# A decode kernel with two cached-attention passes: half of wq and a quarter of wo leave SBUF and are reread, and all 16 chunks of a row's last two units stay on chip between its passes

## The chip, the cores and the metric

The kernel runs on one core of one Trainium2 chip. The metric is the device time of one execution in microseconds (us). The kernel before takes 1079.54 us, the median of three runs (1079.27 to 1081.7). MB is 10^6 bytes, KB in the profile is 1024 bytes.

## What is computed

There are 8 rows (batch entries), each with one token of 448 values. The layers are attention, mixer, attention, mixer, each added to its input:

```python
x = x + A(layernorm(x), k_cache, v_cache, wq, wo)   # pass 0
x = x + B(layernorm(x), w1, w2, w3, w4)
x = x + A(layernorm(x), k_cache, v_cache, wq, wo)   # pass 1, the same caches and weights
x = x + B(layernorm(x), w1, w2, w3, w4)
```

`A` has 16 query heads of 256 and 8 KV heads, two query heads to each KV head, and 4096 cached positions: q = x @ wq, softmax(q k^T / 16) @ v, then @ wo. `B` adds gelu(layernorm(x1) @ w3) @ w4 to x1, where x1 = x + hs. With one token the shifts in `B` push out the only position, so hs is zero and w1 and w2 are not needed; the kernel leaves them out. Both attention passes read the same cache, so what stays on chip after pass 0 of a row need not be read again for pass 1.

## The kernel before, in words

**Units and chunks.** A *unit* is one row, one pass and one pair of KV heads (`gp`, 0 to 3), which serves four query heads. A unit has 4 K chunks and 4 V chunks; a chunk is 128 partitions of 8 KB, 1024 KB in all. So a row has 32 chunks in a pass. The units with gp 0 and 1 are called *free* (heads 0 to 7), those with gp 2 and 3 *kept* (heads 8 to 15).

**Places.** All chunks go through one SBUF tile, `places`, of NC = 15 places of one chunk each (L61, L77). `emit_loads` (L750) walks a fixed list of loads, in the order in which the chunks are used, and issues each on SP's DMA queue as soon as the plan has a place for it; two K chunks in neighbouring places go as one DMA of 2048 KB (L765), a single chunk as one DMA (L790), and a V chunk in `halved` as two DMAs of 512 KB (L793). SP is in order: a load whose place is still in use holds up the loads behind it.

**What stays.** Of the 16 chunks of a row's two kept units, 12 stay in their places from pass 0 to pass 1 (`kept`, L64). One more (`inner`) is moved to four PSUM banks by four VectorE transposes (`away`, L835) and back (`back`, L842), and a quarter of another (`part`) to a fifth bank (L1114, back at L1127), so that 768 KB of it are read again. The weights wq, wo, w3 and w4 are loaded once and stay in SBUF.

**The work on a chunk.** VectorE transposes a K chunk in place in three instructions (`transpose_k`, L803). TensorE makes scores from a pair of K chunks (`scores`, L818) into the PSUM bank `sc`: the first pair into columns 0 to 255, the second into 256 to 511. ScalarE takes the exponential of a pair (`exps`, L827). For a V chunk TensorE runs 16 matmuls (`pv`, L871). K chunks that stayed need no second transpose.

**Order of the work.** `first_kept` and the loop at L639 write the order out by hand, as a list of items, each one chunk. Per row b it is: pass 1 of the row's kept units; then, for the next row, a mix of free units ahead of their turn (`ahead`, L573, three or four units per row, from pass 0 of later rows and from pass 1 of earlier ones) and pass 0 of its two kept units. At the end of this, V chunks that are due (`AFTER` = 11 of them, in `narrow`) are worked one half at a time, and between the halves `step` (L930) advances the *chain* of the row (`chain`, L522): heads 8 to 15 through wo, mixer (`mlp`), and q for pass 1 (`project_q`, L323: 128 matmuls on wq for all 16 heads), after which pass 1 of the row's kept units can start. So the chain stage is the stretch in which only V chunks are worked, with three places left over, and the stretch after it has all K chunks of the row.

**q and wo.** q of pass 0 is projected once for all 8 rows. `spread_q` (L346) writes a row's q for all 16 heads into one of two tiles `qbd`. `first_half` (L512) takes heads 0 to 7 of a row's pass 0 through wo (64 matmuls). For pass 1, rows 0 to 3 go through wo and the mixer together (`rest`, L561), rows 4 to 7 at the end of the kernel (L1136 on).

Of the kernel before, what the change touches and what calls it, by code (L numbers as in the profile page):

```python
# [17 lines left out]
def kernel(  # L18
# [42 lines left out]
    NC = 15  # L61
# [3 lines left out]
    kept += [(GP - 1, 1, n) for n in range(1, 4)] + [(GP - 2, 1, 2)]  # L65
    inner = (GP - 2, 1, 1)
    part = (GP - 1, 1, 0)
    Q4 = 4 * Dh
# [9 lines left out]
    slots = [places_t[:, n * PB : (n + 1) * PB] for n in range(NC)]  # L78

# [50 lines left out]
    def room_ps(what, nb):  # L130

        at, n = {"y": (288, 8), "st": (296, 2), "h": (298, HC), "q": (288, NB2)}[what]
        if nb == 1:
            return misc[:, at : at + n]
        if nb < Bn:
            at = {"y": 352, "st": 384, "h": 400}[what]
            return misc[:, at : at + n * nb]
        at, n = {"y": (0, 8), "st": (64, 2), "h": (80, HC), "q": (256, NB2)}[what]
        return store[0][:, at : at + n * nb]
# [51 lines left out]
    wq_sb = split_tile(HD, "wq_sb")  # L191
    w3_sb = split_tile(F, "w3_sb")
    wo_sb = consts.tile([128, NB2, D], BF16, name="wo_sb")
    w4_sb = consts.tile([128, HC, D], BF16, name="w4_sb")
    qbds = [consts.tile([128, 8, GP, 4, 2], BF16, name=f"qbd{k}") for k in range(2)]
# [29 lines left out]
    def norm(x, nb, twice):  # L225
# [71 lines left out]
        if nb == 1:  # L297
            nc.vector.scalar_tensor_tensor(  # L298
                xbs(1)[:, 0:4, 0], xc[:, :, 0], rl, low[:, int(twice)], ALU.mult, ALU.mult
            )  # L300
            parts = parts[1:2]
        for p0, p1, x0, f0, f1, to in parts:
            pp = slice(x0, x0 + p1 - p0)
            dst = xbs(nb)[p0:p1, to : to + f1 - f0, :]
# [18 lines left out]
    def project_q(b0, nb, qT):  # L323

        yield from norm(xT[:, :, b0 : b0 + nb], nb, False)
        q_ps = room_ps("q", nb).rearrange("p (c b) -> p c b", b=nb)
        for j in range(2):
            for h in range(Hq):
                for fc in range(4):
                    w, xi = wblk(wq_sb, HD, 2 * h + j, fc)  # L330
                    if nb == 1:
                        wide(q_ps[:, j * Hq + h, :], w, xbs(1)[:, xi, :], fc == 0, fc == 3)
                        continue
                    nc.tensor.matmul(
                        q_ps[:, j * Hq + h, :],
                        w,
                        xbs(nb)[:, xi, :],
# [3 lines left out]
                if h % 8 == 7:  # L341
                    yield (3, 0)[j] if h == Hq - 1 else None
        nc.vector.tensor_copy(qT, q_ps)  # L343
        yield

    def spread_q(qT, qbd):  # L346


        qs = misc[0:32, 128 : 128 + 4 * NB2].rearrange("p (e n) -> p e n", e=4)
        for ep in range(4):  # L350
            e2, par = ep // 2, ep % 2
            sel = identb[:, 64 * e2 : 64 * e2 + 64].rearrange("p (j r) -> p r j", r=2)[:, par, :]
            nc.tensor.matmul(qs[:, ep, :], sel, qT, start=True, stop=True)  # L353
# [12 lines left out]
    def out_cols(rhs, w, n, b0, nb, every):  # L366

        y_ps = y_room(nb)[:, 0]
        yield from add_cols(y_ps, rhs, w, range(n), every)
# [3 lines left out]
    def add_cols(y_ps, rhs, w, rows, every, open=None):  # L373

        for fc in range(4):
            at = min(128 * fc, D - 128)
            for i in rows:
# [5 lines left out]
                if open is None and y_ps.shape[-1] == 1:  # L383
                    wide(y_ps[:, fc, :], w[:, i, at : at + 128], rhs(i), start, stop)
# [3 lines left out]
                    w[:, i, at : at + 128],  # L388
# [52 lines left out]
    def mlp(b0, nb):  # L441
        HT = yield from mlp_hidden(b0, nb)
        yield from out_cols(lambda c: HT[:, c, :], w4_sb, HC, b0, nb, 2)
# [67 lines left out]

    def first_half(b, st, ready):  # L512

        OT = work.tile([128, 2, Hq // 2, 1], BF16, tag="OTa", bufs=1)
        yield from half(st["o", 0], st["z"], [0, 1], OT[:, :, :, 0], ready)
        yield from add_cols(
            y_room(1)[:, 0], lambda i: OT[:, i % 2, i // 2], wo_sb, range(NB2 // 2), 2
        )
        xs = xT[:, :, b : b + 1]
        nc.vector.tensor_add(xs, xs, y_room(1)[:, 0])  # L520

    def chain(b, st, ready):  # L522
# [5 lines left out]
            wo_sb,  # L528
# [6 lines left out]
        qT = chn.tile([128, NB2], BF16, tag="qT2", bufs=2)  # L535
        yield from project_q(b, 1, qT[:].unsqueeze(2))
        state[1, b] = {"qT": qT}
        give_q((1, b))

    def first_last(b, st, ready):  # L540

        yield from half(st["o", 1], st["z"], [2, 3], OT2[:, :, Hq // 2 :, b], ready)
        if b == Bn - 1:
# [3 lines left out]
                wo_sb,  # L547
# [9 lines left out]
    def last(b, st, gps, ready):  # L557
        o = st.pop(("o", 0))
        yield from half(o, st["z"], gps, OT2[:, :, 4 * gps[0] : 4 * gps[-1] + 4, b], ready)

    def rest():  # L561

        yield from out_cols(lambda i: OT2[:, i % 2, i // 2, :MID], wo_sb, NB2, 0, MID, 1)
        yield from mlp(0, MID)
        nc.vector.memset(HTw[:, :, 0:MID], 0.0)
        yield

# [4 lines left out]
    REST = keep[0]  # L572
    ahead = [[(0, 1, gp) for gp in free] + [(0, 2, gp) for gp in free]]  # L573
    second = [(1, b, gp) for b in range(Bn - 1) for gp in free]
    for b, n in enumerate((2,) * (Bn - 5) + (1, 1, 3, 3)):
        units = second[:n]
        del second[:n]
        if b + 3 < Bn:
            units += [(0, b + 3, gp) for gp in free]
        ahead.append(units)  # L580
    assert len(ahead) == Bn and not second
# [8 lines left out]
    AFTER = 11  # L590
# [20 lines left out]

    def first_kept(b, units, before):

        k2, k3 = ((0, b, gp) for gp in keep)
        todo = list(units)
        block(todo.pop(0), before)
        if len(todo) > 2:
            block(todo.pop(0))
        block(k2)
# [10 lines left out]
        if n == AFTER:  # L630
# [4 lines left out]

    block((0, 0, free[0]))
    block((0, 0, free[1]), (0, 0, free[0]))
    first_kept(0, ahead[0], (0, 0, free[1]))
    for b in range(Bn):  # L639
# [5 lines left out]
        else:  # L645
            block((1, b, free[0]), k2)
            block((1, b, free[1]), (1, b, free[0]))
            block(None, (1, b, free[1]))
# [14 lines left out]
    loads = [it for it in items if not (tasks[it[0]][0] == 1 and (stays(it) or inside(it)))]  # L663
# [20 lines left out]
    for it in items:  # L684
        if late(it) and it[2] % 2 == 0:
            used_at[it] = used_at[it[0], 0, it[2] + 1]
    again = {(tasks[n][1:], kv, c): k for k, (n, kv, c) in enumerate(items) if tasks[n][0] == 1}
    for b in range(Bn):
        again[(b, keep[0]), 0, 0] = again[(b, inner[0]), *inner[1:]]
    free_at = [-1] * NC  # L690
# [59 lines left out]
    def emit_loads(most=None):  # L750
        n = 0
        while loads and places and n != most:
# [27 lines left out]
            dst = slots[p]  # L780
            rows = (A_v_cache if kv else A_k_cache)[b, 2 * gp : 2 * gp + 2].rearrange(
# [6 lines left out]
            if loads and it not in halved:  # L788
                z0 = Q4 if tasks[t][0] == 1 and halfway(it) else 0
                nc.sync.dma_start(dst[:, z0:], src[:, z0:])  # L790
# [5 lines left out]
            n += 1  # L796
# [8 lines left out]
    def scores(t, x, qbd, gp, also=None, between=None):  # L805
# [3 lines left out]
        for n in range(8):  # L809
# [4 lines left out]
            for k in range(4):  # L814
                v = kv[:, k, 2 * half + e2, par]
                if also is not None:
                    v = bass.AP(v.tensor, v.offset, [v.ap[0], ((also - t) * PB, 2), *v.ap[1:]])
                nc.tensor.matmul(  # L818
                    sc[32 * k : 32 * k + 8, 128 * x : 128 * (x + nx)],
                    qbd[:, ep, gp].rearrange("p a h -> p (a h)"),  # L820
# [5 lines left out]
    def exps(p_sb, zall, gp, u):  # L826
        nc.scalar.activation(  # L827
            p_sb[:, :, :, 2 * u : 2 * u + 2].rearrange("p t i x -> p x t i"),
            sc[:, 256 * u : 256 * u + 256].rearrange("p (x t i) -> p x t i", x=2, t=4),
# [18 lines left out]

    def transpose_p(p_sb, p_to):
# [13 lines left out]
    def pv(o_ps, v, a, gp, r, between):  # L863

        g = 2 * gp + a // 2
        for y in range(16):
            if y == 8 and between is not None:
# [6 lines left out]
                v[:, y * Dh : (y + 1) * Dh],  # L874
# [20 lines left out]
    state = {}  # L895
    x_row = spare[1][:Bn, 256 : 256 + D]
    nc.sync.dma_start(x_row, A_x.rearrange("b s d -> (b s) d"))
    for t, src, cols in ((wq_sb, A_wq, HD), (w3_sb, B_w3, F)):
        nc.sync.dma_start(t[0:64, 3 * cols :], src[384:448, 0 : cols // 2])
        nc.scalar.dma_start(t[64:128, 3 * cols :], src[384:448, cols // 2 :])  # L900
# [391 lines left out]
```

## Time and profile before

| what | value |
|---|---|
| median of three runs | 1079.54 us |
| the profiled execution: first to last instruction | 1076.9 us |
| its time beside the median | 2.6 us less than the median, taken to lie around the span |
| HBM read | 436.28 MB |
| first DMA issued | 0.74 us after the span's start |
| last V chunk worked, to the end of the span | 1065.48 us, 1076.9 us |
| VectorE / TensorE busy | 611.0 us (57%) / 632.9 us (59%) |
| K loads of 2048 KB: number, issue to landing | 65, 19.4 us |
| V loads of 512 KB: number, issue to landing | 202, 7.2 us |

In a row of the view by stretches, "PE busy (x)" and the like are the busy time of an engine and its instructions in that stretch, then come the granted TensorE clock, the DMA share (busy share of the 16 DMA engines; it can read a little above 1) and GB/s. In the waits, "A <- B: total, times, longest" says that A's instructions stood idle until B was done. SPq is the DMA queue that SP issues, with its waits for places.

### The profile page before, as it was taken

The page shows a single profiled execution, that of the slowest core. Times are in us where ns is not written, and L with a number is a line of the kernel's source. Part 1 is how long each engine was busy: PE and PEld are TensorE (multiplying, and loading weights), DVE is VectorE, ACT ScalarE, POOL GpSimd, SP SyncE. Part 2 cuts the span into 40 slices and gives each one's busy share as a digit, 9 for nine tenths or more (in the row PEclk, how much of TensorE's full clock was granted, in tenths as well). Part 3 has the DMA queues.
Part 4 walks back from the last instruction along what each step waited for, and adds up shares of the span by engine and source line. Part 5 has one row for each costly group of instructions (what it writes and reads, how often), then busy time and mean ns, then how long its engine had stood idle before and what let it go on. Part 6 is the DMA issues. An engine that isn't in the chain of part 4 may idle for free.

```text
span 1076.9 us, 29818 instructions
## 1 busy us (share of the span) xinstructions
PE 632.9 (59%) x13292; PEld 398.7 (37%) x13292; DVE 611.0 (57%) x1269; ACT 161.8 (15%) x613; POOL 16.3 (2%) x27
## 2 busy tenths in 40 slices
PE   3244467644775438664476537754675367756785
PEld 2122235422443214442254314532453235433555
DVE  4257841677426872278714773297428653875272
ACT  0001111111111111111112111111111111111110
POOL 0000000000000000000000000000000000000000
PEclk9998557755587555765668655766686568655855
DMA  9999999999999999999999999999999999999995
GB/s 355 392 426 426 425 409 396 423 424 424 388 414 424 425 421 393 415 427 421 421 402 409 424 424 393 395 425 424 412 390 425 425 407 402 424 424 406 390 419 206
DMA packets 69200, 438.22 MB, mean 407 GB/s; under 512 B 7368, under 2 KB 11344, under 8 KB 38736
## 3 DMA queue, kind: packets, MB, share of 16 engines
q1 hardware_dynamic: 68880, 435.94, 98.8%
q8 instruction: 104, 1.70, 0.6%
q10 hardware_dynamic: 192, 0.38, 0.1%
q14 instruction: 24, 0.20, 0.0%
HBM read 436.28 MB, written 0.01 MB: 405 GB/s over the span
## 4 chain that ended last, share of the span: by engine, by line
DMA 65%; PE 18%; DVE 10%; SPq 3%; ACT 2%; issue 2%; POOL 0%; DVEq 0%; ACTq 0%
DMA places<-in_A_v_cache_dram 37%; DMA places<-in_A_k_cache_dram 28%; PE o L871 6%; DVE places L803 6%; PE sc L818 5%; PE misc L170 3%; SPq L189 2%; DVE store L838 1%; ACT p_n L827 1%; SPq L790 1%; PE misc L501 1%; DMA wq_sb<-in_A_wq_dram 1%; DVE places L845 1%; PE misc L854 0%; PE misc L386 0%
## 5 line engine op out<-in xcount | busy, mean ns | idle before, releaser
L803 DVE STREAM_TRANSPOSE places<-places 128x512 uint32<-128x512 uint32 (+1 forms) x576 | 457.9, 855 | 130.3 <-DMA places<-in_A_k_cache_dram 128.5
L818 PE MATMUL sc<-places,qbd 128*8 128x256 bf16 (+1 forms) x4896 | 237.6, 340 | 249.1 <-DVE places L803 240.4
L871 PE MATMUL o<-places,ptw 128*8 128x256 bf16 x3968 | 235.4, 365 | 127.7 <-DMA places<-in_A_v_cache_dram 103.0
L818 PEld LDWEIGHTS <-qbd 128*8 128x8 bf16 x4896 | 124.1, 100 | 327.0 <-DVE places L803 144.9
L871 PEld LDWEIGHTS <-ptw 128*8 128x8 bf16 x3968 | 98.2, 99 | 193.0 <-issue 122.1
L827 ACT ACTIVATE p_n<-sc 128x256 bf16<-128x256 f32 x128 | 94.9, 741 | 383.5 <-PE sc L818 383.5
L981 ACT COPY ptw<-psv 128x32 bf16<-128x32 bf16 x248 | 52.2, 225 | 194.7 <-PE o L871 188.9
L861 ACT CAST psv<-misc 128x128 bf16<-128x128 f32 x64 | 17.0, 266 | 234.4 <-PE misc L854 234.4
L465 DVE RECIPROCAL rz<-misc 128x8 f32<-128x8 f32 (+1 forms) x35 | 6.6, 189 | 71.6 <-PE misc L462 71.6
L357 DVE CAST qbd<-misc 32x64 bf16<-32x64 f32 x104 | 22.4, 216 | 28.0 <-PE misc L353 26.9
L501 PE MATMUL misc<-R_t,o_sb 128*128 128x8 f32 (+1 forms) x132 | 28.2, 323 | 13.7 <-ACT o_sb L495 7.1
L170 PEld LDWEIGHTS <-wq_sb 128*128 128x128 bf16 x1024 | 30.2, 102 | 14.7 <-issue 14.4
L170 PE MATMUL misc<-xb,wq_sb 128*128 128x32 bf16 x1024 | 33.7, 186 | 2.4 <-DVE xb L298 1.3
L501 PEld LDWEIGHTS misc<-R_t,o_sb 128*128 128x128 f32 x132 | 25.3, 267 | 25.3 <-ACT o_sb L495 14.0
L170 PEld LDWEIGHTS <-wo_sb 128*128 128x128 bf16 x1024 | 29.9, 101 | 11.3 <-issue 11.2
L170 PE MATMUL misc<-OT,wo_sb 128*128 128x32 bf16 x1024 | 32.7, 184 | 1.9 <-DVE OT L505 1.7
L827 ACT ACTIVATION_READ_ACCUMULATOR p_n<-sc 128x1 f32 x128 | 33.5, 262 | 0.0
L170 PEld LDWEIGHTS <-w_sb 128*128 128x128 bf16 x896 | 27.0, 101 | 15.0 <-issue 14.2
L343 DVE CAST qT<-misc 128x32 bf16<-128x32 f32 x8 | 1.5, 192 | 50.5 <-PE misc L170 50.5
L497 DVE MEMSET o<- 128x256 f32 x33 | 9.0, 272 | 34.5 <-PE o L871 31.9
L269 POOL TENSOR_TENSOR t<-t,nhalf 128x2 f32<-128x2 f32 (+2 forms) x18 | 12.0, 669 | 983.6 <-DVE t L290 983.6
L854 PEld LDWEIGHTS <-p_n 128*128 128x128 bf16 x256 | 11.7, 104 | 31.7 <-issue 20.2
(137 smaller groups left out, 313.3 us busy)
## 6 DMA issues: line engine op xcount, KB each, us to landing
places<-in_A_k_cache_dram SPq DMA_DIRECT2D x65, 2048.0 KB, 19.4
places<-in_A_v_cache_dram SPq DMA_DIRECT2D x107, 1024.0 KB, 20.7
places<-in_A_v_cache_dram SPq DMA_DIRECT2D x202, 512.0 KB, 7.2
places<-in_A_k_cache_dram SPq DMA_DIRECT2D x62, 1024.0 KB, 13.2
places<-in_A_v_cache_dram SPq DMA_DIRECT2D x8, 768.0 KB, 14.9
wo_sb<-in_A_wo_dram SPq DMA_DIRECT2D x1, 3584.0 KB, 27.9
wq_sb<-in_A_wq_dram SPq DMA_DIRECT2D x3, 1024.0 KB, 9.0
w_sb<-in_B_w_dram SPq DMA_DIRECT2D x1, 1568.0 KB
```

The lines of the kernel that those rows point to most:

```text
L170: nc.tensor.matmul(bass.AP(out.tensor, out.offset, [out.ap[0], (1, WIDE)]), w, x.to_broadcast([128, WIDE]), start=start, stop=stop, skip_g ...
L189: nc.sync.dma_start(t[:, fc * cols : (fc + 1) * cols], src[fc * 128 : fc * 128 + 128, :])
L269: nc.gpsimd.tensor_tensor(rs[:, k0:k1].rearrange("p n b -> p (n b)"), ve[:, k0:k1].rearrange("p n b -> p (n b)"), nhalf[:].to_broadcast([1 ...
L357: nc.vector.tensor_copy(qbd[32 * a : 32 * a + 32, :, :, a, :], qs.rearrange("p e (f g u h) -> p (e f) u g h", f=2, u=2, h=2)[:, :, u],)
L501: nc.tensor.matmul(ot_ps[:, j], o_sb[:].rearrange("p (i j) -> p j i", j=2)[:, j], R, start=True, stop=True)
L803: nc.vector.transpose(w, w)
L818: nc.tensor.matmul(sc[32 * k : 32 * k + 8, 128 * x : 128 * (x + nx)], qbd[:, ep, gp].rearrange("p a h -> p (a h)"), v, start=(n == 0), sto ...
L827: nc.scalar.activation(p_sb[:, :, :, 2 * u : 2 * u + 2].rearrange("p t i x -> p x t i"), sc[:, 256 * u : 256 * u + 256].rearrange("p (x t ...
L854: nc.tensor.matmul(pt_ps[:, t], p_sb[:, t].rearrange("p i x -> p (i x)"), cols, start=True, stop=True,)
L861: nc.scalar.copy(p_to, pt_ps.rearrange("p t k (a h) -> p a (t k) h", a=4))
L871: nc.tensor.matmul(o_ps[32 * q : 32 * q + 8, :], ptz[:, at : at + 8], v[:, y * Dh : (y + 1) * Dh], start=False, stop=(y >= 12), skip_group ...
L981: nc.scalar.copy(ptw[:, ring_of[it], :, 6:8], psv[slot_of[it[0]]][:, it[2]])
```

## The change

- wq of heads 0 to 7 leaves SBUF (`wq_sb` holds heads 8 to 15), and so does wo of heads 0 to 3 (`wo_sb` holds 24 of 32 blocks of 128 rows). They are loaded into places as items of their own kind (`weights`, `load_weights`): wq's half in two places by four DMAs (1024, 512, 128 and 128 KB), wo's quarter in one place by one DMA (896 KB).
- wq's half is loaded for all rows' pass 0, and for pass 1 for the rows 0 to 2, 3 and 4, 5 and 6, and 7: five times. wo's quarter is loaded for pass 0 of row 0, rows 1 and 2, rows 3 to 6, and row 7 (there also for pass 1 of rows 0 to 3), and for pass 1 of rows 4 to 7: five times.
- Heads 0 to 7 of q (`project_rows`) and of wo (`early_rows`) are done for the group of rows at once, in one piece; `project_q` in the chain does heads 8 to 15 alone (64 matmuls). `early_rows` first runs `step` until the rows of its group have been through `half`.
- NC goes from 15 to 17, and 14 chunks stay in places. `inner` is moved to PSUM as before. `part` now stays whole: its first 6 of 16 blocks (1536 of 4096 columns) go to PSUM (four blocks to the fifth bank, two to columns 256 to 511 of `sc`), the other 10 are loaded into a tile of their own, `rest`, and read from there in both passes.
- Both pairs of a unit's scores go to columns 0 to 255 of `sc`.
- `qbd` becomes four tiles of eight heads each; `spread_q` does one half of the heads.
- `ahead` becomes: pass 0 of all rows' free units first, then pass 1 of them, 4, 4, 4, 3, 3, 3, 3, 4 units per row. `AFTER` goes from 11 to 10.

```diff
-    NC = 15
+    NC = 17
-    kept += [(GP - 1, 1, n) for n in range(1, 4)] + [(GP - 2, 1, 2)]
+    kept += [(GP - 1, 1, n) for n in range(1, 4)] + [(GP - 2, 1, n) for n in (0, 2, 3)]
+    PR = 6
+    WI = 8
+    rest_t = consts.tile([128, (16 - PR) * Dh], BF16, name="rest")
-    wq_sb = split_tile(HD, "wq_sb")
+    wq_sb = split_tile(HF, "wq_sb")
-    wo_sb = consts.tile([128, NB2, D], BF16, name="wo_sb")
+    wo_sb = consts.tile([128, NB2 - WI, D], BF16, name="wo_sb")
-    qbds = [consts.tile([128, 8, GP, 4, 2], BF16, name=f"qbd{k}") for k in range(2)]
+    qbds = [consts.tile([128, 8, GP // 2, 4, 2], BF16, name=f"qbd{k}") for k in range(4)]
...
+    def project_rows(w_of, half, r0, r1, ps):
+        nb = r1 - r0
+        for j in range(2):
+            for h in range(HH):
+                for fc in range(4):
+                    w, xi = w_of(2 * h + j, fc)
+                    nc.tensor.matmul(
+                        ps[:, (j * HH + h) * nb : (j * HH + h + 1) * nb],
+                        w,
+                        xb[Bn][:, xi, r0:r1],
...
+    def early_rows(r0, r1, ps, slot):
+        nb = r1 - r0
+        for r in range(r0, r1):
+            while turned.get((ps, r), 0) < (2, 4)[ps]:
+                step(10 * len(items))
...
-    ahead = [[(0, 1, gp) for gp in free] + [(0, 2, gp) for gp in free]]
-    second = [(1, b, gp) for b in range(Bn - 1) for gp in free]
...
+    order = [(0, b, gp) for b in range(1, Bn) for gp in free]
+    order += [(1, b, gp) for b in range(Bn - 1) for gp in free]
+    ahead = []
+    for n in (4, 4, 4, 3, 3, 3, 3, 4):
+        ahead.append(order[:n])
+        del order[:n]
+    q_rows = {3: (0, 3), 5: (3, 5), 7: (5, 7), Bn: (Bn - 1, Bn)}
+    o_rows = {1: (1, 3), 3: (3, 7), 7: (7, 8)}
...
-    AFTER = 11
+    AFTER = 10
...
-            if loads and it not in halved:
-                z0 = Q4 if tasks[t][0] == 1 and halfway(it) else 0
-                nc.sync.dma_start(dst[:, z0:], src[:, z0:])
+            if halfway(it):
+                nc.sync.dma_start(dst[:, 0 : PR * Dh], src[:, 0 : PR * Dh])
+                nc.sync.dma_start(rest_t[:], src[:, PR * Dh :])
+            elif loads and it not in halved:
+                nc.sync.dma_start(dst, src)
...
+    def load_weights(dst, kind, c):
+        if kind == "o":
+            nc.sync.dma_start(
+                dst[:, 0 : WI * D].rearrange("p (h x) -> p h x", x=2 * D),
+                A_wo[0 : WI * 128].rearrange("(h p j) d -> p h (j d)", p=128, j=2),
+            )
+        elif c == 0:
+            nc.sync.dma_start(
+                dst.rearrange("p (f c) -> p f c", f=2),
+                A_wq[0:256, 0:HF].rearrange("(f p) c -> p f c", f=2),
+            )
+        else:
+            nc.sync.dma_start(dst[:, 0:HF], A_wq[256:384, 0:HF])
+            for k in range(2):
+                nc.sync.dma_start(
+                    dst[64 * k : 64 * k + 64, HF : HF + HF // 2],
+                    A_wq[384:448, HF // 2 * k : HF // 2 * (k + 1)],
+                )
...
-                    sc[32 * k : 32 * k + 8, 128 * x : 128 * (x + nx)],
+                    sc[32 * k : 32 * k + 8, 128 * (x % 2) : 128 * (x % 2 + nx)],
-            sc[:, 256 * u : 256 * u + 256].rearrange("p (x t i) -> p x t i", x=2, t=4),
+            sc[:, 0:256].rearrange("p (x t i) -> p x t i", x=2, t=4),
...
+    def part_words(slot):
+        w = slot[:].bitcast(U32)
+        return [
+            (sc[:, 256 : 256 + 128 * (PR - 4)], w[:, 512 : 128 * PR]),
+            (store[4][:], w[:, 0:512]),
+        ]
...
             if (ps, gp, c) == (1, keep[0], 1):
+                where[(b, part[0]), part[1:]] = part_place
+                part_back(slots[part_place])
                 where[(b, inner[0]), inner[1:]] = kept_place
                 back(slots[kept_place])
...
                 if ps == 0 and halfway(it):
-                    nc.vector.transpose(store[4][:].bitcast(U32), slot[:, 0:Q4].bitcast(U32))
+                    part_away(slot)
```

## The prediction

> **What bounds the kernel now.** I read the page's summary and slices first, then its HBM line and chain, then the stretches of one row, last the waits.
>
> ```profile
> span 1076.9 us, 29818 instructions
> ...
> PE 632.9 (59%) x13292; PEld 398.7 (37%) x13292; DVE 611.0 (57%) x1269; ACT 161.8 (15%) x613; POOL 16.3 (2%) x27
> ...
> DMA  9999999999999999999999999999999999999995
> GB/s 355 392 426 426 425 409 396 423 424 424 388 414 424 425 421 393 415 427 421 421 402 409 424 424 393 395 425 424 412 390 425 425 407 402 424 424 406 390 419 206
> ...
> HBM read 436.28 MB, written 0.01 MB: 405 GB/s over the span
> ...
> DMA 65%; PE 18%; DVE 10%; SPq 3%; ACT 2%; issue 2%; POOL 0%; DVEq 0%; ACTq 0%
> ```
>
> No engine is over 59% busy, the DMA engines are busy in every slice but the last, and the rate has a plateau of 424 GB/s with a dip about once a row. The chain of work that ended last is 65% DMA. Where the dips come from is seen in one row:
>
> ```profile
> 281.00:311.00 30.00, 23.71 (x528) 15.41 (x521) 6.30 (x35) 3.22 (x15) 1.25 (x2) 0.65 1.01 389
> 314.00:404.00 90.00, 44.76 (x868) 26.29 (x862) 66.45 (x105) 14.57 (x53) 0.00 (x0) 0.62 1.01 423
> ```
>
> The first is a chain stage: with three places left, loads follow the release of places, and the rate is 389. Over the 4 us stretches of all eight chain stages the shortfall against 424 sums to about 18 us. The second is the rest of a row, at the plateau. There the engines wait for the loads:
>
> ```profile
> DVE places L803 <- DMA places<-in_A_k_cache_dram: 128.5, 64, 16.4
> PE o L871 <- DMA places<-in_A_v_cache_dram: 103.0, 91, 6.0
> ```
>
> Together 231.5 us, some 29 us per row. So time is bytes over rate: 436.28 MB at 424 is 1029 us; 18 us of chain stages, 11 us from the last V chunk to the end (1065.5 to 1076.9) and about 5 us at the start bring it to 1063; the rest is weights and lesser dips.
>
> **Bytes removed.** Pass 1 of a row rereads no chunk of its kept units, where it now rereads 2.75 (two V chunks whole, 768 KB of `part`). Over 8 rows that is 22 chunks of 1.0486 MB, 23.07 MB. They lie in the stretch after the chain, at 424: 2.473 us each, **-54.4 us**.
>
> **Bytes added.** Five loads of wq's half (1.835 MB) and of wo's quarter (0.9175 MB), of which one each stands for the load made now: four of each more, 7.34 and 3.67 MB. The nearest rows are the weight loads at the start:
>
> ```profile
> 8.00:20.00 12.00, 4.35 (x132) 4.02 (x132) 1.33 (x6) 0.00 (x0) 0.00 (x0) 1.00 1.02 423
> 24.00:36.00 12.00, 5.15 (x128) 2.82 (x118) 7.76 (x11) 1.75 (x5) 0.00 (x0) 1.00 1.04 384
> ```
>
> The first holds wq in runs of 8 KB, the second mostly wo, in the runs of 1792 B that it keeps. wq's half has runs of 4 KB and, in the two pieces of 128 KB, of 2 KB; V halves have 4 KB too, but only at the chain stage's 389. So wq costs 17.3 us (at 424) to 18.9 (at 389); I take 17.5, near the first row, since the rereads don't lie in the chain stage. wo costs 8.7 (424) to 10.5 us (351, the lowest 4 us of the start's weights); I take 9.6, at 384. Together **+27.1 us**; net **-27.3 us**, for 12.06 MB less.
>
> **Costs taken at nothing, with their cover.**
> - `part` to PSUM and back: now one transpose of 128x512 each way, 0.684 us; then also one of half the size, some 0.35 us. VectorE has 23.5 us idle in the 90 us above. The move away stands before the chain stage, where the freed place feeds SP: the waits have "SPq L793 <- DVE store L1114: 40.6, 8, 5.1". If all of it shows, 8 x 0.35 = 2.8 us; in that stretch (272 to 280 us) the rate is still 419 to 420, so I take 0.
> - One score region in place of two: the second pair must wait for the first pair's exponential. In the compiled order of the kernel before, the second pair of the first unit already waits for ScalarE, and the trace shows it as "ACT p_n L827: 4.7, 5" ahead of L818: 4.7 us in all. Between 0 and 1.2 us (the longest) for each of the 16 kept units of pass 1, 19 us; VectorE or DMA makes TensorE wait far longer there (240.4 us for L803), so 0.
> - `sc` holding `part`: VectorE, TensorE and ScalarE now share a bank. The Trainium skill, PSUM — Partial Sum Buffer, PSUM bank collisions, says to guard by bank and quadrant and not by address, so the 16 added transposes and the scores exclude each other. Were TensorE the bound, the sum would be 16 x 0.35 = 5.6 us more; by the waits it is not.
> - Heads 0 to 7 in groups: 360 fewer matmuls in all, but in pieces of 64 that nothing is put between, 2 us each (32 take 0.99 us), eleven of them. Behind one on TensorE wait the next scores; K loads take 19.4 us from issue to landing there, so the queue has work for the 2 us. Four more `spread_q` (30 for 26), some 1.5 us of TensorE and VectorE each, in the same cover. Without it all this is 28 us. The forced `step` runs finish what is finished soon anyway: 0.
> - The chain loses two of four q pieces and one of eleven V chunks. Its shortfall of 2.3 us per row may shrink by a tenth (-1.8 us); its front, where the dip is deepest (366 GB/s from 281 to 296), is unchanged. 0.
> - Start and end: the end's order of the last eight V chunks is the same; the start loads the same weights around the same five K chunks. 0.
>
> **Sum.** 1076.9 - 27.3 = 1049.6 us of span, and with the 2.6 us around it **1052.2 us**. The bounds of the loads' rates and the chain are -3.0 and +5.1 us (1049 to 1057).
>
> **Rivals.**
>
> *VectorE sets the pace after the chain* (1075 us). In the new list of loads, 10 to 14 K chunks follow each other after the chain, now four or five before a V chunk comes. A K chunk takes VectorE 2.43 us:
>
> ```profile
> 382.64 4.74 DVE L803 STREAM_TRANSPOSE places<-places 128x1024 uint32<-128x1024 uint32 x6 [2.60 <-DMA places<-in_A_k_cache_dram]
> 387.60 2.43 DVE L803 STREAM_TRANSPOSE places<-places 128x1024 uint32<-128x1024 uint32 x3 [0.22 <-DMA places<-in_A_k_cache_dram]
> ```
>
> against 2.473 of load, so twelve give back 0.5 us, while the moves back from PSUM (four of 0.68, now also 1.0) put 3.7 in: a lag of 3.2 us, which no V chunk makes up. In seven rows 22 us. For it: the rows above show waits of a fraction of a us. Against: about ten places are open in that stretch, 24 us of loads; it decides only if the lag passes the spare ones.
>
> *The rereads stand on the path* (1082 us, no change). A place given to weights frees none until TensorE reaches them; if the queue ran dry at each of the eight rereads, each would show issue to landing on an empty queue, 3.8 us ("wq_sb<-in_A_wq_dram ACTq DMA_DIRECT2D x1, 256.0 KB, 3.8"): 30 us, the gain gone. Against: they are issued among K loads with 19.4 us in hand. A rule goes the same way. The Trainium skill, DMA: Bandwidth & Descriptors, Anatomy of one DMA, gives each DMA a fixed 2.0 us beside its bytes (for GpSimd's path); by it the 20 DMAs of the rereads would cost 40 us if none overlapped, 1092 in all. The trace speaks against paying it: 16 V halves went out in 28.3 us from 271.8 us on, 1.8 us apart, though each takes 7.2 us to land.
>
> *The chain stage starves* (1088 us, slower). It runs on three places in both kernels, but its first load waits for the longer move of `part`, that chunk comes as two DMAs, and its last K chunks come behind any lag. If each stage ran at 338 GB/s (288 to 292 us, the worst 4 us of this row) in place of 389, its 11.7 MB would take 34.5 us for 30: 36 us over eight rows, +9 net. The gain is gone where a stage grows by 27.3 / 8 = 3.4 us. For it: 121.0 us of SPq waits for L871. Against: the stage has the same places and less TensorE work.
>
> That the change doesn't do what it says is excluded by the list of loads of the changed kernel, which has the rereads and no load of kept chunks in pass 1.
>
> **How the numbers follow.** Forecast 0.80, VectorE's pace 0.06, rereads on the path 0.05, starved chain 0.09. A change of 0.3%, 3.2 us, is about what a measurement can tell from none. Faster is the first two cases, 0.86; same is the third, 0.05; slower 0.09. The range takes the forecast's bounds, a little more on the fast side for chain stages that shrink, and on the slow side half of VectorE's case: 1046 to 1066; what is left out is the other cases, 0.2.
>
> **What would show it.** HBM read falls to 424.2 MB. In the stretches after the chain the rate stays at 423 or 424, with dips to about 384 where wo comes in. VectorE's and TensorE's waits for loads fall from 231 us by some 20, as loads stop being late by less. The eight chain stages keep about 389 and 30 us. Wrong would be: long SPq waits on the K transposes together with a DMA share under 0.95 (VectorE's pace), TensorE waiting for `places` from wq or wo with a rate dip there (rereads), or chain stages below 370 GB/s throughout.

## The result and the profile after

The changed kernel takes 1064.26 us (median of four runs, 1061.72 to 1067.2) where the kernel before takes 1079.4 in the same comparison: ratio 0.9864, 95% interval 0.9838 to 0.989. It is faster, by 15 us; 27 were forecast. The time lies inside the range, near its slow end. From the page of the changed kernel:

```profile
span 1059.6 us, 29163 instructions
...
PE 627.0 (59%) x12932; PEld 395.0 (37%) x12932; DVE 616.4 (58%) x1319; ACT 161.7 (15%) x613; POOL 16.4 (2%) x27
...
DMA  9999999999999999999999999999999999999994
GB/s 300 387 424 424 424 415 388 422 421 423 401 406 426 424 420 404 409 403 424 414 389 426 425 410 410 378 425 412 401 424 423 393 389 420 423 418 348 393 416 203
...
HBM read 424.22 MB, written 0.01 MB: 400 GB/s over the span
...
DMA 47%; DVE 24%; PE 21%; ACT 3%; issue 2%; SPq 2%; POOL 1%; DVEq 0%; ACTq 0%
```

The bytes are the forecast 424.2 MB, but the mean rate fell from 405 to 400 GB/s. The chain that ended last was 65% DMA and 10% VectorE; it is now 47% and 24%. The shortfall against 424 GB/s, summed over 4 us stretches of the span, grew from 43.2 to 54.4 us. The 12.06 MB less are worth 28.4 us at 424; 11.2 of them went into this shortfall, and 17.2 remain, which is the 17.3 us between the two spans. This is bookkeeping and names no cause. The profiled execution is the fastest of the four (1061.72 us); in the repeat below, profiled in its slowest execution, the shortfall is 58.5 us.

The waits of the changed kernel (in us: total, times, longest):

```profile
DVE places L902 <- DMA places<-in_A_k_cache_dram: 81.0, 38, 20.1
...
PE o L986 <- DMA places<-in_A_v_cache_dram: 70.9, 75, 5.8
...
DVE sc L958 <- ACT p_n L926: 12.6, 8, 1.6
```

The waits for loads fell from 231.5 to 151.9 us, by 80 where "some 20" were forecast: far more than the 27 us of loads saved would explain. The third line is new. Some stretches of the changed kernel (columns as before; the last two are DMA share and GB/s):

```profile
284.00:300.00 16.00, 12.02 (x296) 8.38 (x296) 4.32 (x25) 1.48 (x8) 0.90 (x2) 0.89 1.00 378
316.00:405.00 89.00, 46.52 (x849) 27.39 (x849) 68.31 (x113) 15.40 (x59) 0.00 (x0) 0.60 1.01 422
...
438.00:526.00 88.00, 48.10 (x950) 30.50 (x950) 59.63 (x105) 13.90 (x55) 0.00 (x0) 0.63 1.01 415
456.00:460.00 4.00, 2.65 (x79) 1.96 (x67) 1.13 (x2) 1.00 (x4) 0.00 (x0) 0.74 1.09 305
...
956.00:972.00 16.00, 12.81 (x292) 8.82 (x284) 3.44 (x19) 2.35 (x11) 0.70 (x1) 0.71 0.86 305
996.00:1000.00 4.00, 3.40 (x53) 2.11 (x53) 0.49 (x3) 0.80 (x3) 0.00 (x0) 0.50 1.03 283
```

An early chain stage (284 to 300) and the stretch after it are nearly as before. The largest new dips are where rereads lie (438 to 526, with 305 at 456; 283 at 996), in the last row's chain stage (956 to 972), and at the start (336 GB/s over the first 48 us, 368 before: 3.6 us).

### The profile page after: what moved, and what is told of

Read it like the earlier page. It is cut to its first block, busy times and chain, and to the rows that moved or that the text cites. A ratio compares the mean times of both kernels' runs of the same rounds, so it can differ in the third digit from the quotient of the medians.

```text
span 1059.6 us, 29163 instructions
## 1 busy us (share of the span) xinstructions
PE 627.0 (59%) x12932; PEld 395.0 (37%) x12932; DVE 616.4 (58%) x1319; ACT 161.7 (15%) x613; POOL 16.4 (2%) x27
## 4 chain that ended last, share of the span: by engine, by line
DMA 47%; DVE 24%; PE 21%; ACT 3%; issue 2%; SPq 2%; POOL 1%; DVEq 0%; ACTq 0%
DMA places<-in_A_v_cache_dram 25%; DMA places<-in_A_k_cache_dram 20%; DVE places L902 18%; PE sc L917 9%; PE o L986 7%; ACT p_n L926 2%; PE misc L174 2%; DMA places<-in_A_wq_dram 2%; PE misc L529 1%; DVE store L937 1%; DVE places L944 1%; DVE qbd L376 1%; SPq L193 1%; SPq L870 1%; ACT o_sb L523 1%
## 5 line engine op out<-in xcount | busy, mean ns | idle before, releaser
L917 PE MATMUL sc<-places,qbd 128*8 128x256 bf16 (+1 forms) x5024 | 246.9, 347 | 244.9 <-DVE places L902 236.1
L986 PE MATMUL o<-places,ptw 128*8 128x256 bf16 x3808 | 232.3, 369 | 101.4 <-DMA places<-in_A_v_cache_dram 70.9
L917 PEld LDWEIGHTS <-qbd 128*8 128x8 bf16 x5024 | 130.4, 104 | 327.8 <-DVE places L902 140.1
L986 PEld LDWEIGHTS <-ptw 128*8 128x8 bf16 x3968 | 103.7, 102 | 171.4 <-issue 95.8
L376 DVE CAST qbd<-misc 32x32 bf16<-32x32 f32 x128 | 23.2, 182 | 27.6 <-PE misc L370 26.3
L529 PE MATMUL misc<-R_t,o_sb 128*128 128x8 f32 (+1 forms) x132 | 26.7, 311 | 20.7 <-DVE R_t L515 13.9
L529 PEld LDWEIGHTS misc<-R_t,o_sb 128*128 128x128 f32 x132 | 23.8, 252 | 30.9 <-issue 17.2
L174 PEld LDWEIGHTS <-w_sb 128*128 128x128 bf16 x896 | 27.3, 103 | 14.2 <-issue 13.8
L490 PE MATMUL misc<-zm,one 128*128 128x8 f32 (+1 forms) x70 | 17.1, 317 | 18.9 <-DVE zm L482 17.1
L490 PEld LDWEIGHTS misc<-zm,one 128*128 128x128 f32 x70 | 14.1, 251 | 29.1 <-issue 24.9
L969 PE MATMUL misc<-identb,p_n 128*128 128x32 bf16 x256 | 18.0, 190 | 9.3 <-ACT p_n L926 6.8
L937 DVE STREAM_TRANSPOSE store<-places 128x512 uint32<-128x512 uint32 x32 | 19.8, 686 | 0.0
L944 DVE STREAM_TRANSPOSE places<-store 128x512 uint32<-128x512 uint32 x32 | 19.7, 672 | 0.0
```

What stands on the lines that cost most here:

```text
L174: nc.tensor.matmul(bass.AP(out.tensor, out.offset, [out.ap[0], (1, WIDE)]), w, x.to_broadcast([128, WIDE]), start=start, stop=stop, skip_g ...
L376: nc.vector.tensor_copy(qbd[32 * a : 32 * a + 32, :, :, a, :], qs.rearrange("p e (f g u h) -> p (e f) u g h", f=2, u=2, h=2)[:, :, u],)
L490: nc.tensor.matmul(z_ps, ones, zm[:], start=True, stop=True)
L529: nc.tensor.matmul(ot_ps[:, j], o_sb[:].rearrange("p (i j) -> p j i", j=2)[:, j], R, start=True, stop=True)
L917: nc.tensor.matmul(sc[32 * k : 32 * k + 8, 128 * (x % 2) : 128 * (x % 2 + nx)], qbd[:, ep, gp % 2].rearrange("p a h -> p (a h)"), v, start ...
L937: nc.vector.transpose(store[n][:].bitcast(U32), slot[:].bitcast(U32)[:, 512 * n : 512 * n + 512])
```

## The experiments

All runs, with the ratio to the kernel before and its 95% interval. Where differences of ratios are given in us below, they are taken of 1078.5 us.

| run | what | median, us | ratio |
|---|---|---|---|
| after_again | the changed kernel | 1064.1 | 0.9867 [0.985, 0.9885] |
| e1_start | wo's load first among the weights | 1064.9 | 0.9867 [0.9848, 0.9885] |
| e2_nobytes | eight rereads keep places, load nothing | 1051.0 | 0.9741 [0.9723, 0.9759] |
| e3_noplaces | eight rereads gone, places too | 1044.6 | 0.9683 [0.9664, 0.9701] |
| e4_light_after | changed, a third of K transposes' instructions out | 1061.8 | 0.9849 [0.9828, 0.9871] |
| e5_light_before | the same in the kernel before | 1077.8 | 0.9997 [0.9984, 1.001] |
| e6_before_22 | kernel before without the 22 chunks | 1027.1 | 0.9534 [0.9511, 0.9558] |
| e7_light_e3 | e3 with e4's edit | 1032.4 | 0.9586 [0.9569, 0.9604] |
| e8_start | small loads of the start on ScalarE's queue | 1064.6 | 0.9881 [0.9861, 0.9901] |
| e9_row7 | e3 with before's spread of free units | 1046.3 | 0.972 [0.9695, 0.9745] |
| e10_scalar_moves | moves to PSUM and back on ScalarE | 1062.1 | 0.9865 [0.9844, 0.9886] |
| e11_both | e8 and e10 together | 1058.9 | 0.9814 [0.9801, 0.9828] |

**The changed kernel again, and the order of its start.** e1 moves one load:

```diff
+    nc.sync.dma_start(wo_sb...)
     for t, src, cols in ((wq_sb, A_wq[:, HF:], HF), (w3_sb, B_w3, F)):
...
     load_split(wq_sb, A_wq[:, HF:], HF)
-    nc.sync.dma_start(wo_sb...)
```

> The changed kernel once more, beside the next three on one chip: 1064 us, about 15 us under the kernel before (1061 to 1067).

> Only the order of the loads at the start is changed: wo_sb's load (2688 KB) goes out straight behind the first five K chunks, ahead of the small pieces of wq_sb and w3. Theory A, that some 4 us of the missing gain are lost at the start because only small loads are under way from 20 to 28 us (240 to 358 GB/s): 2 to 4 us faster than the changed kernel, with 380 GB/s or more from 20 to 28 us. Rival, that the start's loss is made up later or comes from the first 12 us: within 1 us.

The repeat agrees with the first result. e1 changed nothing: its dip only moved, from 24 to 28 us to 28 to 36 us. So the order of wo and the small pieces is not what makes the start slow; that one of its two dips comes from the small pieces themselves, e8 shows below.

**What the rereads cost.** In e2 the eight rereads after the first two keep their places but move no bytes; heads 0 to 7 of those rows then go through whatever the place holds. In e3 the items take no place either, and the same matmuls read weights that lie in SBUF (wrong ones).

```diff
-                load_weights(dst, gp, c)
+                if tasks[t][1] in ((0, Bn), (0, 1)):
+                    load_weights(dst, gp, c)
```

```diff
+    def gone(it):
+        return it[1] == 2 and tasks[it[0]][1] not in ((0, Bn), (0, 1))
...
-        return tasks[it[0]][0] == 1 and (stays(it) or inside(it) or halfway(it))
+        return gone(it) or tasks[it[0]][0] == 1 and (stays(it) or inside(it) or halfway(it))
```

> The eight rereads move no bytes: their items keep their places and TensorE works on what lies there (old chunks in place of weights, so heads 0 to 7 are projected with wrong weights). Theory, that a reread costs its bytes at the rate of the nearest rows: 27 us faster than the changed kernel, 1037. Rival, that the rereads cost more than their bytes by the queue running dry around them: 31 us or more, 1033.

> The eight rereads are left out with their places; the same matmuls run at the same points on the weights that are in SBUF (heads 8 to 15 of wq and other rows of wo, so the values are wrong). If holding three places costs nothing: the same as without the bytes, within 1 us. If the places that the rereads hold are what stops the loads: another 3 to 6 us faster.

e2 came out where neither theory had it: the bytes cost 13.6 us, though at 424 GB/s they are 26.0. e3 came out at the theory that the places stop the loads, a little above its 3 to 6 us: another 6.3. Together the rereads cost 19.8 us. So without any reread the rest of the change gains 34 us and not 54: most of the missing gain was not in the rereads at all. How held places stop the loads is seen in e2. SP issues nothing from 435.2 to 453.2 us, waiting for K transposes and for TensorE's work on V chunks, and the loads under way run out:

```profile
448.00:452.00 4.00, 1.42 (x12) 1.01 (x5) 2.24 (x3) 0.91 (x5) 0.00 (x0) 0.50 0.56 231
452.00:456.00 4.00, 3.43 (x96) 2.64 (x95) 2.82 (x6) 0.64 (x3) 0.00 (x0) 0.50 0.49 152
```

In the changed kernel the weights' own bytes fill most of this stretch. SP's queue there (start, duration, line, what it loads):

```profile
444.45 0.38 SPq L885 DMA_DIRECT2D places<-in_A_wq_dram  x1
444.88 0.47 SPq L890 DMA_DIRECT2D places<-in_A_wq_dram  x1
445.39 1.12 SPq L892 DMA_DIRECT2D places<-in_A_wq_dram  x2
447.09 0.39 SPq L880 DMA_DIRECT2D places<-in_A_wo_dram  x1
455.44 3.26 SPq L839 DMA_DIRECT2D places<-in_A_k_cache_dram  x2
```

Three places go to weights, then SP issues nothing for 8 us. Such a wait need not cost anything: the kernel before has one of 13.1 us (232.7 to 245.8 us) at 406 to 440 GB/s. Here the rate is 400 or more until 456 us and 305 in the 4 us behind, some 1.1 us lost. So the 6.3 us are the price of holding places that bring no bytes; how the 19.8 us divide between bytes and places while both are there, these runs do not tell.

**VectorE's pace.** The last of the three transposes of each K chunk is left out (the scores of its columns are wrong), 110 us less VectorE in each kernel.

```diff
-        for e0, e1 in ((0, 2), (2, 3), (3, 4)):
+        for e0, e1 in ((0, 2), (2, 3)):
```

> The third of the three transposes of every K chunk is left out in the changed kernel (192 instructions of 0.669 us, 128 us of VectorE; the scores of a quarter of each K chunk are wrong). Theory B, that VectorE sets the pace in the runs of 10 to 14 K chunks and the last chain stages start behind it: 5 us or more faster than the changed kernel, and the dip of 247 to 329 GB/s at the last chain gone. Rival, that only loads decide: within 1.5 us.

> The same transpose left out in the kernel before. Theory B says the K runs there are four or five long and VectorE keeps up: at most 2 us faster than before. Rival, that VectorE costs the same in both: as much as in the changed kernel.

In the kernel before it is worth nothing, in the changed one 2 us, within the intervals. As the one cause of the missing 12 us VectorE falls. e4's chain that ended last is back at 66% DMA and 9% VectorE, and yet the time hardly moved: the shares of that chain do not say what a lighter engine is worth.

**The price of the chunks, by itself.** e6 takes the 22 chunks out of the kernel before and leaves all else:

```diff
+    def gone(it):
+        n, kv, c = it
+        return tasks[n][0] == 1 and (tasks[n][2], kv, c) in ((keep[0], 1, 0), (keep[0], 1, 3))
...
-        p = where[(b, gp), (kv, c)] if kept_now else where[it]
+        if gone(it):
+            p = where[(b, gp), (1, 2)]
+        else:
+            p = where[(b, gp), (kv, c)] if kept_now else where[it]
```

> The kernel before, with the 22 chunks alone taken away: in pass 1 of a row's kept units the two V chunks that are reread whole are neither loaded nor given a place (their matmuls read the place of the kept chunk between them, which is freed at the last of the three), and the 768 KB of part keep their place but are not loaded. The values of these chunks in pass 1 are wrong; all matmuls, transposes and exponentials stay, and so do the order of the work, the weights in SBUF and the 15 places. HBM read should be 413.2 MB, as in the run without rereads. Theory 1, the price of 2.473 us a chunk is right and the changed kernel gives it back by other things it does (its start, its order, its chain stages): 54.4 us less than before, 1024 us, at most 3 us off. Theory 2, the price is too high because the stretches after the chain cannot go faster by that much, whatever the order (VectorE and TensorE take what the loads give): near the run without rereads, 1040 to 1047 us, that is 32 to 39 us gained. Between 1028 and 1039 both have a part.

> The changed kernel without its eight rereads and their places (as in the run before it, 1044.6 us), and with the last of the three transposes of every K chunk left out, some 0.6 us of VectorE a chunk and 110 to 128 us in all; the scores of those columns are wrong. Theory VectorE: once fewer loads are left, VectorE's work after the chain is what ends last in the later rows (its chain of waits has 30% VectorE), so the dips at 624 to 668, 720 to 732 and 920 to 956 us go, 12 to 18 us, and the time is 1027 to 1033 us. Theory loads and places: the dips come from three open places in the chain stages and from the start, which a lighter VectorE does not change: 1041 to 1044 us, as the same edit gave 2.4 us in the changed kernel and nothing in the one before.

e6 gains 50.3 us, 4 less than Theory 1 had, so the price of a chunk nearly stands (2.29 us where 2.473 was taken). The theory that the kernel cannot go that fast falls: e6 has the same 413.21 MB as e3 and takes 16 us less. e7 says what stands between the two for the larger part: with a lighter VectorE e3 becomes 10 us faster (by the ratios; the medians, taken on two chips, give 12), the low end of what that theory expected. So VectorE does end last in e3, where fewer loads are left to wait for. Whether e6 would gain by the same edit was not run. The chains by engine of e6, e3 and e7:

```profile
DMA 49%; PE 23%; DVE 20%; SPq 3%; issue 2%; ACT 2%; POOL 0%; DVEq 0%; ACTq 0%
```

```profile
DMA 38%; DVE 30%; PE 24%; ACT 3%; issue 3%; SPq 2%; POOL 1%; DVEq 0%; ACTq 0%
```

```profile
DMA 53%; PE 24%; DVE 14%; ACT 3%; issue 3%; SPq 3%; POOL 1%; ACTq 0%; DVEq 0%
```

e6 and e3 run the same K transposes, and in runs that are nearly as long: behind a chain stage SP loads up to 13 K chunks without a V chunk between them in e6 and up to 14 in e3, where the kernel before has up to 4. So the long runs of K chunks alone do not make the difference. What VectorE has more in e3 is the second piece of `part`, and that is no matter of 0.35 us. These are the two moves of that piece in e3, each once per row (count, busy us, mean ns, then idle time of VectorE just before them and who ended it), and then the move of `part` in the kernel before:

```profile
L961 DVE STREAM_TRANSPOSE sc<-places 128x256 uint32<-128x256 uint32 x8 | 3.7, 460 | 12.6 <-ACT p_n L929 12.6
L965 DVE STREAM_TRANSPOSE places<-sc 128x256 uint32<-128x256 uint32 x8 | 3.6, 450 | 13.7 <-ACT ptw L1111 7.7 <-ACT p_n L929 6.0
```

```profile
L1127 DVE STREAM_TRANSPOSE places<-store 128x512 uint32<-128x512 uint32 x8 | 5.5, 688 | 0.0
L1114 DVE STREAM_TRANSPOSE store<-places 128x512 uint32<-128x512 uint32 x8 | 5.5, 684 | 0.0
```

The piece that goes to `sc` waits for ScalarE both ways, 26.3 us in 16 moves, and VectorE's queue waits with it; the move of `part` before waited for nothing. SP in turn waits longer for the move away in e3 (first line) than in e6:

```profile
SPq L876 <- DVE store L961: 57.6, 8, 10.6
SPq L804 <- DVE store L1128: 40.9, 8, 5.3
```

The longest of these waits, 10.6 us, is in the last row of e3, where the move comes at the end of 40 us of K transposes. The stretches of e3 there, and the last chain stage of e6:

```profile
920.00:928.00 8.00, 5.55 (x136) 3.99 (x135) 7.60 (x16) 0.92 (x4) 0.00 (x0) 0.50 0.49 178
928.00:944.00 16.00, 8.67 (x224) 5.13 (x216) 15.36 (x21) 2.75 (x8) 0.00 (x0) 0.61 1.00 405
944.00:960.00 16.00, 12.21 (x272) 8.38 (x269) 4.12 (x20) 3.15 (x13) 0.70 (x1) 0.71 0.78 264
```

```profile
940.00:956.00 16.00, 13.23 (x290) 8.80 (x289) 3.61 (x20) 2.73 (x13) 0.70 (x1) 0.71 1.02 394
```

VectorE is busy for 7.6 of 8 and 15.4 of 16 us, and the loads starve twice: at 178 GB/s, where SP waits 8.5 us for K transposes, and at 264 behind the move, where e6 keeps 394. No run takes the second piece alone away, so its share of e3's loss is not shown. e7 keeps all 16 moves and their waits (31.5 us) and is within 5.6 us of e6, which suggests that they cost much only where VectorE is behind with its K transposes.

**The order of the free units.** e9 is e3 with the spread of the kernel before.

```diff
-    for n in (4, 4, 4, 3, 3, 3, 3, 4):
+    for n in (4, 4, 4, 4, 3, 3, 3, 3):
-    q_rows = {3: (0, 3), 5: (3, 5), 7: (5, 7), Bn: (Bn - 1, Bn)}
+    q_rows = {3: (0, 3), 5: (3, 5), 6: (5, 6), 7: (6, 7), Bn: (Bn - 1, Bn)}
```

> The changed kernel without its eight rereads and their places (1044.6 us; the heads that used them take weights that lie in SBUF, so their values are wrong), and with the free units spread over the rows as in the kernel before: 4, 4, 4, 4, 3, 3, 3, 3 in place of 4, 4, 4, 3, 3, 3, 3, 4. The changed kernel cannot do that with its groups, since pass 1 of rows 5 and 6 needs q of row 6, which is there only after row 6's chain; here that costs one more piece of 64 matmuls and no load. Theory order: the four units in row 7 keep VectorE busy without a gap until the last chain stage (40 us of K transposes up to 944 us), the move of part stands behind them and the loads starve at 920 to 956 us, 11 us of shortfall; with three units that falls to 3 or 4 and the time to 1036 to 1038 us. Rival, the place of the units does not matter and VectorE's lag only moves to another row: 1042 to 1046 us.

The theory falls. With three units in the last row it loses as much (12.5 us of shortfall from 920 to 1000 us, 12.1 in e3). How the units are spread is not the cause.

**Two edits that keep the whole computation.** e8 sends the six small loads of the start by ScalarE's queue; e10 makes all moves to PSUM and back copies on ScalarE; e11 has both.

```diff
-        nc.sync.dma_start(t[0:64, 3 * cols :], src[384:448, 0 : cols // 2])
+        nc.scalar.dma_start(t[0:64, 3 * cols :], src[384:448, 0 : cols // 2])
...
-                nc.sync.dma_start(
+                (nc.sync if now[0] else nc.scalar).dma_start(
                     dst[64 * k : 64 * k + 64, HF : HF + HF // 2],
...
-            nc.vector.transpose(kept_words.bitcast(U32), words)
+            nc.scalar.copy(kept_words, words)
...
-            nc.vector.transpose(words, kept_words.bitcast(U32))
+            nc.scalar.copy(words, kept_words)
```

> The changed kernel with the same loads, but the six small ones of its start (128 and 112 KB: the last 64 rows of wq in both halves and of w3) issued on ScalarE's queue, the four for SBUF ahead of all others; SP's queue then has x, the 1024 and 512 KB of wq, the five K chunks, and the weights. Theory start: the shortfall of 0 to 48 us (9.5 us, where the kernel before has 6) comes from these small loads standing in SP's line, first at 4 to 12 us, then at 23 to 27 us, where the rate is 200; it falls to 6 or less and the time by about 3 us, to 1061 us. Rival: the start waits for something else that moves with the order (as when wo went ahead of the pieces: the dip moved to 28 to 36 us and the time stayed): 1064 us.

> The changed kernel with all moves to PSUM and back (16 of the whole chunk, in four pieces each, 32 of part) as copies on ScalarE, which is 15% busy, in place of transposes on VectorE; nothing is left out. That takes some 58 us from VectorE (8 rows with 2.46 x 2 and 1.14 x 2 us), and the move of part no longer waits on VectorE's queue for ScalarE's exponential (12.6 us in 8 times) or behind K transposes. Theory VectorE's queue: SP's waits for the moves (45.4 us) fall by half or more, the chain stages' dips shrink by 0.5 us or more each, 1056 to 1060 us. Rival, the stage is held by TensorE and the three places, as the lighter VectorE's 2.4 us suggested: 1062 to 1065 us.

> The changed kernel with both edits that took a little off its own shortfall, and nothing left out: the six small loads of the start on ScalarE's queue (1.4 us less shortfall from 0 to 48 us), and the moves to PSUM and back as copies on ScalarE (58 us less VectorE). If the two losses stand in a row, the gains add up: 2 to 4 us less than the changed kernel, 1060 to 1062 us. Rival, what is won at the start or on VectorE is lost at the next chain stage, where three places and TensorE hold the loads: 1063 to 1065 us, as with each edit alone.

Alone, neither shows: e8 is at 0.9881 and e10 at 0.9865, where the changed kernel has 0.9867. Both did what they were to do, though. The stretch from 16 to 28 us of the changed kernel, and of e8:

```profile
16.00:28.00 12.00, 5.35 (x128) 3.02 (x127) 9.87 (x13) 1.48 (x4) 0.00 (x0) 1.00 1.02 339
```

```profile
16.00:28.00 12.00, 6.05 (x161) 4.39 (x162) 8.76 (x16) 0.74 (x2) 0.00 (x0) 1.00 1.01 408
```

So the second dip of the start does come from the small loads in SP's line; the first one, 8 to 16 us (355 in the changed kernel, 335 in e8, 421 before), does not, and its cause stays open. In e10 VectorE's 616.4 us fell to 563.3 and SP hardly waits for the move of `part` any more (1.9 us). Its waits for TensorE's work on V chunks grew by as much, though; the changed kernel, then e10:

```profile
SPq L873 <- PE o L986: 92.6, 136, 3.1
...
SPq L873 <- DVE store L958: 45.4, 7, 8.3
```

```profile
SPq L873 <- PE o L982: 143.1, 133, 6.7
```

So TensorE stood right behind VectorE there. Together the two edits gain 5.7 us on the changed kernel: 0.9814, with an interval clear of all three. "What is won is lost at the next stage" holds for each alone and falls for both. That two losses lay beside each other, the late loads of the start and VectorE's late moves, so that taking one away leaves the other, would fit; no run shows it. From the page of e11, and the last chain stage of e11 and of e10:

```profile
PE 617.3 (59%) x12932; PEld 391.5 (37%) x12932; DVE 563.1 (53%) x1223; ACT 205.0 (19%) x709; POOL 16.3 (2%) x27
...
HBM read 424.22 MB, written 0.01 MB: 402 GB/s over the span
...
DMA 51%; PE 23%; DVE 17%; ACT 4%; issue 3%; SPq 1%; POOL 1%; DVEq 0%; ACTq 0%
```

```profile
956.00:972.00 16.00, 12.80 (x287) 8.54 (x287) 4.06 (x24) 1.42 (x7) 0.75 (x2) 0.71 0.98 370
```

```profile
956.00:972.00 16.00, 14.15 (x314) 9.36 (x307) 3.25 (x19) 2.13 (x10) 0.70 (x1) 0.66 0.99 379
```

With the same bytes, the stage that ran at 305 GB/s runs at 370. But it does so in e10 alone too, so what e11 has over e10 lies elsewhere: of the 4.0 us between their profiled spans 1.6 are in the first 48 us and 1.8 from 48 to 920. e11 is the fastest version here that computes everything, 20 us below the kernel before.

## Why the prediction was right in direction and 12 us off in size

The gain was forecast as a sum, and the runs give its terms, in the order in which they were taken away here (another order would divide them otherwise, since they overlap):

| term | forecast, us | measured, us | from |
|---|---|---|---|
| 22 chunks | -54.4 | -50.3 | e6 against before |
| everything taken at nothing | 0 | +16.1 | e3 against e6, equal bytes |
| rereads | +27.1 | +19.8 | after against e3 |
| sum | -27.3 | -14.4 | |

- **The step that failed is "Costs taken at nothing, with their cover".** It is the term furthest off, 16.1 us where 0 was taken. Its cover was VectorE's idle time ("VectorE has 23.5 us idle in the 90 us above") and the loads being late; with the 22 chunks gone VectorE ends last in e3, by 10 us (e7). Inside it two items:
  - *"`part` to PSUM and back ... 2.8 us; so I take 0."* The instruction was sized nearly right (0.46 us, forecast 0.35), the wait before it was not seen. The piece shares `sc` with the scores, and waits for ScalarE; in the changed kernel the 16 moves hold up VectorE's queue for 26.7 us (12.6 away, 14.1 back). The prediction looked at the region from TensorE's side, where its 0 is right: the scores' wait for the exponential rose from 4.7 to 5.3 us. By the Trainium skill, PSUM — Partial Sum Buffer, PSUM bank collisions, PSUM is to be guarded by bank and quadrant and not by address. The trace agrees in that there are waits between the engines that share the bank; but they are 26.7 us, on VectorE, where the prediction priced the exclusion at 16 x 0.35 = 5.6 us, on TensorE. Whether the hardware asks for these waits or only the program's order does, no run here tells apart. What they cost in time is not shown by itself: e10, which takes all moves off VectorE, gains nothing alone and 7.2 us with e8's start in place (e11 against e8).
  - *"Start and end: ... the start loads the same weights around the same five K chunks. 0."* The same weights come in more and smaller loads: in SP's line two of 128 KB stand ahead of the first K chunk, one of 128 and one of 112 KB behind the fifth. The changed start cost 3.6 us of shortfall in the first 48 us. e8 takes back 1.9 of them (10.0 to 8.1 us) and is no faster, so its price in time is not shown either.
- **Smaller slips in the same list.** The upper bound of +5.1 us holds the 2.8 us of `part`'s move beside the loads' rates. The trace has 128 casts into `qbd`, four to each `spread_q`: 32 calls and not 30; VectorE's time for them rose only from 22.4 to 23.2 us.
- **"22 chunks ... -54.4 us" held to 8%.** e6's chain stages give back a little more than before; its one profiled execution was the slowest of its runs, so the 4 us are not placed further.
- **"Together +27.1 us" was too much.** At the plateau's rate the bytes alone are 26.0 us, and bytes and places together cost 19.8, so the rule that a byte costs its time was off: e3 falls short by 64.1 us and the changed kernel by 54.4 (58.5 in the repeat), so 6 to 10 us of the bytes fill time that was lost anyway. That held places can stop the loads the prediction had as a rival and put nothing in the sum for; without the bytes they cost 6.3 us. By the Trainium skill, DMA: Bandwidth & Descriptors, Anatomy of one DMA (GpSimd's path), the 20 loads of the rereads would have cost 40 us if none overlapped, an estimate; nothing of that kind is seen in 19.8 us for bytes, places and all.
- **The rivals.** *VectorE sets the pace* had the right engine and, for the changed kernel, the wrong size: 2 us by e4, not 22. A lag of VectorE that the loads do not make up, as it had, is what e3 and e7 show; that the moves behind the K transposes make it is argued from the traces. *Rereads stand on the path* happens in the small: TensorE waits for wq at 459 to 460 us, at 305 GB/s, and 2.4 us in all for the four rereads of wq. *The chain stage starves* happens in one row of eight, at 305 GB/s where 338 was the point taken, which is why it took some 4 us and not the gain.
- **The signs named.** Bytes: right. Rate after the chains: 415 to 422, lowest where rereads lie, where 423 or 424 was said. Waits for loads: by 80 us instead of 20, which was the plainest sign that something else had become late. "A DMA share under 0.95" as the mark of VectorE's pace was a bad choice: the share stayed at 1.01 where the rate had fallen to 415, and only in the last row's chain stage did a stretch of 16 us read less than 0.95 (0.86). SP's waits on K transposes, the other half of that sign, rose from 110.2 to 127.6 us.
- **The range.** That the time lies inside it is in part luck. Of the 16.1 us that were taken at nothing, 7.3 are set off by rereads that cost less than priced, and the slow end that holds the result was there for half of VectorE's case, which e4 sizes at 2 us in this kernel.

What stays open: the first dip of the start, and how the 16.1 us divide between VectorE, the start and the groups' pieces. By e7, the start's 4 us of shortfall and VectorE's 10 would make up most of it, but the kernel of e6 was not run with a lighter VectorE, and neither the second piece of `part` nor the groups' pieces were taken away alone.

## What to carry to other kernels

A sum of bytes at the plateau's rate is good for the bytes alone; each edit "taken at nothing" is covered only as long as the loads are late, and taking bytes away removes that cover (here leaving out a third of the K transposes' instructions was worth nothing in the kernel before, 2 us in the changed one and 10 in e3). When a buffer is put into a bank or a tile that others use, price the wait on both sides, on the queue of the engine that moves as well as on the engine that computes. If two small edits show nothing alone, run them together before dropping them.

## What the runs showed of the hardware that was not expected

- The DMA share does not always show a low rate: it reads 1.02 at 339 GB/s (16 to 28 us), 1.09 at 305 (456 to 460 us) and 1.03 at 283 (996 to 1000 us) in the changed kernel, but 0.86 at 305 (956 to 972 us). The GB/s column does.
- Small loads (112 and 128 KB, to 64 partitions each) made a dip larger than their bytes: with two of them in SP's line behind the K chunks, 24 to 28 us ran at 240 GB/s; with all six on ScalarE's queue the same 4 us ran at 395 (e8), though the time stayed.
- A copy of 128x512 32-bit words between SBUF and PSUM takes ScalarE 0.58 us out and 0.59 to 0.63 us back (e10), less than VectorE's transpose of the same words (0.69 and 0.67 us), and a piece of 128x256 back 0.42 us (0.45).
